# Six small edits at the seams of a two-layer-type network: the root's chain kept together, a padding and some loads and stores moved between engines

## The chip, the cores and the metric

The kernel runs on one core of a Trainium2 chip. A core has a matrix engine (TensorE, PE in the profile; PEld are its weight loads), a vector engine (VectorE, DVE), an activation engine (ScalarE, ACT), a general engine (GpSimd, POOL) and a sequencer for transfers (SyncE, SP). SP, ACT and POOL each have a queue into which they issue DMA transfers, and the transfers of all of them run on the core's 16 DMA engines. The metric is the device time of one execution in microseconds (us); the time before is the median of three runs, 2985.52 us (2983.61 to 2987.02).

## The reference, cut to what matters

The input is a sequence of 2048 positions with 640 channels. Four layers follow one another, each with a layer norm in front and a residual add behind: a long convolution (A), a multi-query attention (B), and the same two again with the same weights.

```python
x = A_u
x = x + _A_ref(_layernorm(x), ...)      # y = irfft(rfft(u, 2L) * rfft(K, 2L))[:L] + u * Dskip
x = x + _B_ref(_layernorm(x), wq, wk, wv, wo)
x = x + _A_ref(_layernorm(x), ...)      # the same K
x = x + _B_ref(_layernorm(x), wq, wk, wv, wo)

def _layernorm(x, axis=-1, eps=1e-5):
    m = jnp.mean(x, axis=axis, keepdims=True); v = jnp.var(x, axis=axis, keepdims=True)
    return (x - m) / jnp.sqrt(v + eps)

# A: K[d, l] = Re sum_n C[d,n] * exp(dt[d] * A[d,n] * l) * dt[d] * B[d,n],   128 states n, 2048 steps l
# B: 32 query heads of 20 channels, one key head and one value head of 20 channels
#    softmax(q k^T / sqrt(20)) v, the heads joined, times wo (640 x 640)
```

## The kernel before, in words

**Stages.** `kgen` makes the convolution kernel K in 20 units and writes it to the tensor `kd` in DRAM. `conv_layer` transforms K once into a spectrum (`kernel_spectra`, first layer only), then transforms x in five chunks of 128 channels, multiplies, and transforms back into `self.x`, which stays on the chip throughout ([128 partitions, 16 tiles, 640 channels]). `_attn` projects x to q, k and v in four blocks of 512 rows, then `main_loop` goes over 4 blocks (nb) x 8 head groups of four heads (hg) x 16 key tiles (t). Layers are called a, b, c, d.

**Order.** Tile, the layer that the kernel is written in, places each instruction by a planner with a cost model; inside a `manual_schedule` block the named engines keep the order in which the program writes them. The convolution is written out for PE, ACT and DVE; `kgen`'s loop too; `main_loop` for PE and ACT; `prepare(0)` of the attention for ACT and DVE (L1193). Everything else, the queues of SP and POOL among it, is in the planner's order. An engine runs its instructions in order: a waiting one holds up those behind it.

**The end of `kgen` (L567 to L569).** After unit 20 is begun, the tables' memory is released and `conv_weights` (L585) loads the forward transform weights `wf`, eight transfers of 512 KB, in GpSimd's queue. [...] SP's queue has the stores of K (L499): eight after unit 15, eight after the last unit.

**The end of a convolution (L957 to L1003).** When chunk 3 is under way, ScalarE computes mean and variance over the first 384 channels (`stats_first`, sums over an activation); in the first layer the attention's weights are split on the way into a high and a low part (`attn_weights`, six pieces: piece 0 are key and value weights in the padded tile `kv`, pieces 1 to 5 rows of wq; a first half casts and multiplies on PE, a second half writes the low part). Four `turn`s add the last chunk's inverse transform, four tiles at a time. After each turn `stats_last` takes bn_stats over the last 256 channels of these four tiles and aggregates them (eight operations); `norm_part` joins both parts and makes scale and shift. Its `root` (L734) is one square root on ACT and five dependent DVE operations, of which the reciprocal is the first, and one more product gives the shift. For block 0 (`norm_part(0, 1)`) the first six operations run after turn 0, and the other six are woven one by one between the eight operations of `stats_last(1)` (L998, L999).

**The start of an attention.** `prepare(nb)` normalizes four tiles on ACT (L1117), transposes them on PE in groups of two, two and one column blocks of 128 (L1128), copies the result to `xh` rounded (L1132, ACT) and the rest to `xl` (`low`, L1135, DVE). `norm_part(1, 3)`, the scale of blocks 1 to 3, stands around the first `low` of block 0. `project(nb)` multiplies with high and low weights (L1152), 15 matmuls for each of six column blocks, evicts q (L1164 to L1166), and calls `prepare(nb + 1)` at the third. `ob`, cast at L1098, is the operand that sums squares per head (L1179).

**The main loop.** Each step multiplies scores, exponentiates on ACT (L1286) and multiplies with the values (L1296). When a head group ends it is normalized, its rows go by DMA into `ot` chunks of 128 channels, and each chunk complete by then puts eight units (nb, k, u) on the list `later`. At t = 8 of each head group `later` moves to `queue`, and at t = 2, 5, 8, 11 and 13 one unit is taken from it: a product with `wo` on PE (L1356) and an add on DVE (L1344). What is left after the last step is multiplied in the tail. In layer d a tile that is complete is stored, one half by SP and one by GpSimd (L1351).

Of the kernel before, what the change touches and what calls it, by code (L numbers as in the profile page):

```python
# [11 lines left out]
F32 = mybir.dt.float32  # L12
# [3 lines left out]
AF = mybir.ActivationFunctionType  # L16
# [5 lines left out]
P = 128  # L22
# [173 lines left out]
class Net:  # L196
# [154 lines left out]
    def _kgen(self, ctx):  # L351
        tc, nc, ins = self.tc, self.nc, self.ins
# [152 lines left out]
        n = len(units)  # L505
        engines = {mybir.EngineType.PE, mybir.EngineType.Activation, mybir.EngineType.DVE}
        with tc.manual_schedule(engines=engines):
            for h in range(2):
                phase(0, h)
            for u in range(n + 3):  # L510
                now, nxt, prod, tot = u < n, u + 1 < n, 0 < u <= n, 2 <= u < n + 2
                odd = u % 2 == 1
                if u >= 3:
                    store(u - 3)
                if now and not odd:
                    trig(u, 0)
                if prod:
                    products(u - 1, 0)
                if now:
                    sizes(u, 0)  # L520
                    if odd:
                        exps(u, 0)
                if nxt:
                    phase_first(u + 1, 0)
                if tot:
                    sums(u - 2, range(0, 2))
                if now:
                    sizes(u, 1)
                    if odd:
                        exps(u, 1)  # L530
                if tot:
                    sums(u - 2, range(2, 3))
                if nxt:
                    phase(u + 1, 0)
                if now and odd:
                    sizes(u, 2)
                    exps(u, 2)
                if prod:
                    products(u - 1, 1)
                if now:  # L540
                    trig(u, 0 if odd else 1)
                if tot:
                    sums(u - 2, range(3, 5))
                if nxt:
                    phase(u + 1, 1)
                if prod:
                    products(u - 1, 2)
                if tot:
                    sums(u - 2, range(5, 7))
                if now:  # L550
                    if odd:
                        trig(u, 1)
# [12 lines left out]
                for t in {n: range(8, 12), n + 1: range(12, 16)}.get(u, ()):  # L565
                    self.stats(t)
                if u == n:  # L567
                    early.close()
                    self.conv_weights(nc.gpsimd)  # L569

    def conv_setup(self, ctx):
        tc = self.tc
# [110 lines left out]

    def stats_setup(self, nm):

        self.sm = {n: self.cvp.tile([P, 16], F32, name=f"sm{n}{nm}") for n in ("sum", "shift", "sq", "base")}
        self.mvb = self.cvp.tile([P, 16, 2], F32, name=f"mvb{nm}")

    def stats_first(self, g, dump):

# [102 lines left out]
    def conv_layer(self, nm, first):  # L793
# [7 lines left out]
        with tc.manual_schedule(engines={mybir.EngineType.PE, mybir.EngineType.Activation,  # L801
# [193 lines left out]
            for g in range(4):  # L995
                if g > 0:
                    turn(g)
                among = part[6:] if g == 1 else ()  # L998
                weave(self.stats_last(g), [(min(n + 1, 8), a) for n, a in enumerate(among)])  # L999
                if g == 0:  # L1000
                    part = self.norm_part(0, 1)
                    for call in part[:6]:
                        call()  # L1003
# [9 lines left out]
    def attn_weights(self, scr, fresh):  # L1013
# [11 lines left out]
                nc.sync.dma_start(w, dst.rearrange("p (k n) -> p k n", k=5))  # L1025
            return []
        kv = wp.tile([P, 5, 52], F32, name="kv")
        nc.gpsimd.memset(kv, 0.0)
        nc.sync.dma_start(kv[:, :, 0:20], ins["B_wv"].rearrange("(k p) n -> p k n", p=P))
        nc.sync.dma_start(kv[:, :, 32:52], ins["B_wk"].rearrange("(k p) n -> p k n", p=P))  # L1030
        minus = scr[:, 2688:2816]
# [27 lines left out]
                for w, dst in parts:  # L1059
                    nc.sync.dma_start(dst.rearrange("p (k n) -> p k n", k=5), w)  # L1060

        return [(lambda k=k: first(k), lambda k=k: second(k)) for k in range(6)]

    def attn_layer(self, nm, out=None):
        with ExitStack() as ctx:
# [16 lines left out]
    def _attn(self, ctx, nm, out):  # L1082
# [12 lines left out]
        ob = ap.tile([P, 6, 64], F32R, name="ob")  # L1095
        obr = ap.tile([P, 6, 64], F32, name="obr")
        nc.sync.dma_start(obr.rearrange("p m h -> p (m h)"), ins["c_ob"])
        nc.vector.tensor_copy(ob, obr)  # L1098
        nc.sync.dma_start(self.mxd.rearrange("h r n -> (h r) n"), ins["c_row"])
        nc.sync.dma_start(kt[1:66:64].bitcast(F32), self.mxd[32])  # L1100
        self.qps = {}
# [1 line left out]
        with tc.tile_pool(name=f"pj{nm}", bufs=1, reuse_waits="tile") as pj:  # L1103
# [7 lines left out]
            def prepare(nb):  # L1111

                xs = []
                for i in range(4):
                    t = 4 * nb + i
                    x = pj.tile([P, D], F32, tag="x", bufs=4, name=f"x{nb}{i}")
                    nc.scalar.activation(x, self.x[:, TAUS[t]], AF.Identity, scale=self.rs[:, t : t + 1],  # L1117
                                         bias=self.nmr[:, t : t + 1])
                    xs.append(x)
                if nb > 0:  # L1120
                    xhs[nb] = pj.tile([P, 5, 512], F32R, tag=f"xh{nb % 2}", bufs=1, name=f"xh{nb}")
                xh = xhs[nb]
                xl = xls[nb] = pj.tile([P, 5, 512], F32R, tag="xl", bufs=2, name=f"xl{nb}")
                for k0, n in ((0, 2), (2, 2), (4, 1)):
                    pt = self.ps2(f"pt{nm}{nb}{k0}")
                    for k in range(n):
                        for i in range(4):
                            nc.tensor.transpose(pt[:, 512 * k + 128 * i : 512 * k + 128 * i + 128],  # L1128
                                                xs[i][:, 128 * (k0 + k) : 128 * (k0 + k) + 128], self.ident)
                    hi, lo = xh[:, k0 : k0 + n], xl[:, k0 : k0 + n]  # L1130
                    pv = pt[:, 0 : 512 * n].rearrange("p (k c) -> p k c", k=n)
                    nc.scalar.activation(hi, pv, AF.Copy)  # L1132

                    def low(hi=hi, lo=lo, pv=pv):
                        nc.vector.tensor_tensor(lo, pv, hi.bitcast(F32), ALU.subtract)  # L1135

                    weave([low], [(0 if n < 6 else 1, a) for n, a in enumerate(
                        self.norm_part(1, 3) if nb == k0 == 0 else ())])

            def project(nb):  # L1140
                cols = slice(512 * nb, 512 * nb + 512)
# [48 lines left out]
                    call()  # L1190
                nc.vector.reduce_max(nrm[:, nb : nb + 1], pn, axis=AX.X)

            with tc.manual_schedule(engines={mybir.EngineType.Activation, mybir.EngineType.DVE}):  # L1193
                prepare(0)
            for nb in range(4):
                project(nb)
# [48 lines left out]
    def main_loop(self, ap, mp, kt, vt, nm, out):  # L1245
# [93 lines left out]
        def add(nb, u, py, last):  # L1339
# [7 lines left out]
            if out is None:  # L1347
                self.stats(t)
            else:
                for jh, eng in enumerate((nc.sync, nc.gpsimd)):  # L1350
                    eng.dma_start(self.rows(out)[jh][:, t], self.x[64 * jh : 64 * jh + 64, t])  # L1351

        def product(py, o, w, u, m, start, stop):
# [2 lines left out]
                nc.tensor.matmul(py[j : j + m], o[:, 128 * i + j : 128 * i + j + m],  # L1356
                                 w[:, 320 * half : 320 * half + 320], start=start, stop=stop)

        def projection(t):

            if t == 8:
                queue.extend(later)
                later.clear()
            if t in (2, 5, 8, 11, 13) and queue:
# [5 lines left out]
        with tc.manual_schedule(engines={mybir.EngineType.PE, mybir.EngineType.Activation}):  # L1370
# [3 lines left out]
            for s, step in enumerate(steps):  # L1374
# [4 lines left out]
                projection(t)  # L1379
# [110 lines left out]
```

## Time and profile before

One execution was profiled: 2985.19 us, with a span of 2983.4 us from the first to the last instruction. DVE, ACT, PE are busy times in us; the last two columns are the granted TensorE clock and the mean busy share of the DMA engines.

| stage | from, to (us) | PE | DVE | ACT | PE clock | DMA |
|---|---|---|---|---|---|---|
| kernel K | 0 to 284.6 | 169.04 | 265.66 | 226.36 | 0.67 | 0.31 |
| to the first spectrum matmul | 284.6 to 301.4 | 8.32 | 13.49 | 10.74 | 0.67 | 0.93 |
| spectra, convolution a | 301.4 to 602.9 | 280.66 | 285.46 | 112.38 | 0.97, 0.93 | 0.57, 0.46 |
| seam to attention b | 602.9 to 610.2 | 4.96 | 6.72 | 5.79 | 1.00 | 0.01 |
| projection b | 610.2 to 712 | 99.51 | 30.13 | 44.64 | 1.00 | 0.37 |
| main loop b | 722 to 1667 | 940.37 | 260.12 | 942.05 | 1.00 | 0.11 |
| projection d | 1906.5 to 2008.5 | 99.62 | 30.10 | 44.63 | 1.00 | 0.37 |
| main loop d | 2018 to 2964.7 | 941.95 | 244.09 | 942.16 | 1.00 | 0.11 |
| tail | 2964.7 to 2983.4 | 12.09 | 8.23 | 0.00 | 0.96 | 0.23 |

Over the span PE is busy 2774.5 us (93%), ACT 2425.9 (81%), DVE 1373.9 (46%), POOL 91.6 (3%). These shares are means over stages with different limits. A row of a timeline gives the start, the duration, the engine, the line, the operation and its tiles (buffer numbers left out, so both layers' tiles differ only in the letter behind the name), and in brackets how long the engine stood idle before it and what ended that. Matmuls are pipelined, so a PE row's end is modelled. SPq and POOLq rows are issues of transfers, not the transfers.

### The profile page before, as it was taken

How to read it: one execution, taken by the hardware profiler on the slowest of the kernel's cores; microseconds unless marked ns; L12 is line 12 of the kernel's file. 1: busy time of each engine (PE TensorE's matmuls, PEld its weight loads, DVE VectorE, ACT ScalarE, POOL GpSimd, SP SyncE). 2: the span in 40 equal slices, each digit the busy share in tenths (PEclk: the TensorE clock that was granted, in tenths of full speed). 3: DMA queues.
4: the chain of work that ended last, by engine and by line, in shares of the span. 5: the costliest groups of instructions: out<-in, count | busy, mean ns of one | idle time of the engine just before them, and what ended most of it. 6: DMA issues, size and time to landing. Idle time of an engine off the chain costs nothing. (4 is left out here: it accounts for less than half of the span.)

```text
span 2983.4 us, 52547 instructions
## 1 busy us (share of the span) xinstructions
PE 2774.5 (93%) x21712; PEld 1262.1 (42%) x21712; DVE 1373.9 (46%) x1800; ACT 2425.9 (81%) x2904; POOL 91.6 (3%) x153
## 2 busy tenths in 40 slices
PE   1776989998999999999999998899999999999999
PEld 0333978775232333333232687762233232323323
DVE  7999899942223222323232599721222222222222
ACT  5888243455999999999999634339999999999997
POOL 0001001100000000000000011000000000000000
PEclk9655999999999999999999999999999999999999
DMA  6113555533201010101100256231010101100100
GB/s 145 35 17 92 194 166 113 138 102 106 82 22 27 21 28 20 28 22 25 24 24 20 88 113 161 64 128 43 22 27 25 42 21 27 41 24 25 40 19 23
DMA packets 128112, 177.70 MB, mean 60 GB/s; under 512 B 59524, under 2 KB 84100, under 8 KB 124244
## 3 DMA queue, kind: packets, MB, share of 16 engines
q1 hardware_dynamic: 102680, 137.70, 16.1%
q0 software_dynamic: 23216, 35.55, 6.0%
q8 instruction: 175, 2.87, 0.4%
q10 hardware_dynamic: 1968, 0.98, 0.1%
q14 instruction: 73, 0.60, 0.1%
HBM read 95.22 MB, written 48.04 MB: 48 GB/s over the span
## 5 line engine op out<-in xcount | busy, mean ns | idle before, releaser
L1286 ACT ACTIVATE pt<-scd 128x1024 f32<-128x1024 f32 x1024 | 942.2, 1115 | 7.5 <-DMA qpd<-mxd 4.1
L1286 ACT ACTIVATE pt<-scb 128x1024 f32<-128x1024 f32 x1024 | 942.2, 1116 | 7.5 <-PE scb L1282 5.9
L1296 PE MATMUL pod<-pt,vt 128*32 128x512 f32 x4096 | 547.2, 606 | 4.4
L1296 PE MATMUL pob<-pt,vt 128*32 128x512 f32 x4096 | 547.0, 606 | 4.4
L1282 PE MATMUL scb<-qpb,kt 62*128 62x512 f32 x2048 | 386.0, 451 | 6.1 <-PEq L1231 5.7
L1282 PE MATMUL scd<-qpd,kt 62*128 62x512 f32 x2048 | 386.3, 452 | 5.7 <-DVEq L1231 5.3
L1282 PEld LDWEIGHTS scd<-qpd,kt 62*128 62x128 f32 x2048 | 166.1, 185 | 401.8 <-ACT pt L1286 392.9
L1282 PEld LDWEIGHTS scb<-qpb,kt 62*128 62x128 f32 x2048 | 166.0, 185 | 402.1 <-ACT pt L1286 392.5
L1344 DVE TENSOR_TENSOR x<-pyd,x 128x320 f32<-128x320 f32 x146 | 71.8, 492 | 561.0 <-PE pyd L1356 561.0
L1344 DVE TENSOR_TENSOR x<-pyb,x 128x320 f32<-128x320 f32 x146 | 71.8, 492 | 547.4 <-PE pyb L1356 547.4
L1316 DVE RECIPROCAL rc<-rc 128x512 f32<-128x512 f32 x62 | 207.9, 3353 | 2.1
L1296 PEld LDWEIGHTS pod<-pt,vt 128*32 128x32 f32 x4096 | 80.7, 108 | 178.3 <-issue 160.3
L1296 PEld LDWEIGHTS pob<-pt,vt 128*32 128x32 f32 x4096 | 80.6, 108 | 178.2 <-issue 160.1
L1356 PE MATMUL pyb<-wo,ot 128*32 128x320 f32 x1168 | 105.3, 432 | 0.0
L1356 PE MATMUL pyd<-wo,ot 128*32 128x320 f32 x1168 | 105.3, 432 | 0.0
L654 PE MATMUL za<-xna,wf 128*128 128x256 f32 x384 | 86.9, 389 | 4.9 <-ACT xna L821 4.9
L654 PE MATMUL zc<-xnc,wf 128*128 128x256 f32 x384 | 85.8, 385 | 5.0 <-ACT xnc L821 5.0
L1313 DVE COPY on<-pod 128x512 f32<-128x512 f32 x31 | 21.4, 691 | 136.1 <-PE pod L1296 122.1
L445 PE MATMUL pe<-kg,tm 48*128 48x512 bf16 (+1 forms) x120 | 61.1, 612 | 24.0 <-ACT m L453 15.3
L1313 DVE COPY on<-pob 128x512 f32<-128x512 f32 x31 | 21.4, 692 | 131.4 <-PE pob L1296 108.9
L654 PEld LDWEIGHTS za<-xna,wf 128*128 128x128 f32 x384 | 74.5, 195 | 16.6 <-ACT xna L821 6.2
L654 PEld LDWEIGHTS zc<-xnc,wf 128*128 128x128 f32 x384 | 73.7, 193 | 16.4 <-ACT xnc L821 6.2
(372 smaller groups left out, 3188.9 us busy)
## 6 DMA issues: line engine op xcount, KB each, us to landing
Akh<-kh SPq DMA_DIRECT2D x10, 2048.0 KB
kh<-Ak SPq DMA_DIRECT2D x5, 2048.0 KB
qhd<-qh SPq DMA_DIRECT2D x40, 256.0 KB
qld<-ql SPq DMA_DIRECT2D x40, 256.0 KB
qpb<-qhd SPq DMA_DIRECT2D x256, 40.0 KB
qpd<-qhd SPq DMA_DIRECT2D x256, 40.0 KB
ot<-on SPq DMA_DIRECT2D x216, 40.0 KB
wf<-in_c_wf POOLq DMA_DIRECT2D x16, 512.0 KB, 7.8
```

The source lines that it names most:

```text
L445: nc.tensor.matmul(pe[:, 512 * h : 512 * h + 512], grp(tm, u, par, rows), kg[0:rows, col : col + 512], start=True, stop=True)
L654: nc.tensor.matmul(zv[:, :, c, kk], self.wf[:, t + 4 * h, j, c, kk], x, start=(n == 0), stop=(n == 3))
L1282: nc.tensor.matmul(sc[:, 512 * par : 512 * par + 512], kt[rows, 128 * t : 128 * t + 128], qps[nb, hg, pr][rows], start=True, stop=True)
L1286: nc.scalar.activation(pt, sc, AF.Exp, scale=SCALE)
L1296: nc.tensor.matmul(po[32 * j : 32 * j + 32], vt[:, t], pts[step, j // 2][:, 512 * (j % 2) : 512 * (j % 2) + 512], start=(t == 0), stop=(t ...
L1313: nc.vector.tensor_copy(on, po)
L1316: nc.vector.reciprocal(rc, rc)
L1344: nc.vector.tensor_tensor(xh, py, xh, ALU.add)
L1356: nc.tensor.matmul(py[j : j + m], o[:, 128 * i + j : 128 * i + j + m], w[:, 320 * half : 320 * half + 320], start=start, stop=stop)
```

## The change

Six edits, in the order of the program:

- the forward weights `wf` are loaded in SP's queue at the end of `kgen`, not in GpSimd's (the second load, inside the first attention loop, stays in GpSimd's);
- the tiles of the statistics are allocated in the pool that lives on through the attention, and `stats_last(3)` moves into `prepare(0)`: two bn_stats ahead of the first `low` and two behind it, the aggregates behind the third `low`, then `norm_part(1, 3)`, then the cast of `ob`;
- of block 0's `norm_part`, the six operations from the reciprocal on run together ahead of `stats_last(1)`;
- the tile `kv` is no longer filled with zeros by GpSimd; ScalarE writes zeros into the twelve columns that no load fills; the six pieces are taken in the order 1, 2, 0, 3, 4, 5;
- the transposes of `prepare` go tile by tile, not column block by column block, and PE is among the engines whose order is kept for `prepare(0)`;
- in the last block of the main loop `later` moves to `queue` at t = 5, and the stores of the last block's second halves are issued by ScalarE.

```diff
-                    self.conv_weights(nc.gpsimd)
+                    self.conv_weights(nc.sync)
...
-        self.sm = {n: self.cvp.tile([P, 16], F32, name=f"sm{n}{nm}") for n in ("sum", "shift", "sq", "base")}
-        self.mvb = self.cvp.tile([P, 16, 2], F32, name=f"mvb{nm}")
+        self.sm = {n: self.xp.tile([P, 16], F32, tag=f"sm{n}", bufs=1, name=f"sm{n}{nm}") for n in ("sum", "shift", "sq", "base")}
+        self.mvb = self.xp.tile([P, 16, 2], F32, tag="mvb", bufs=1, name=f"mvb{nm}")
...
                 among = part[6:] if g == 1 else ()
-                weave(self.stats_last(g), [(min(n + 1, 8), a) for n, a in enumerate(among)])
+                if g < 3:
+                    weave(self.stats_last(g), [(0, a) for a in among])
...
-        nc.gpsimd.memset(kv, 0.0)
+        nc.scalar.activation(kv[:, :, 20:32], self.ident[:, 0:60].rearrange("p (k n) -> p k n", k=5),
+                             AF.Copy, scale=0.0)
...
-        return [(lambda k=k: first(k), lambda k=k: second(k)) for k in range(6)]
+        return [(lambda k=k: first(k), lambda k=k: second(k)) for k in (1, 2, 0, 3, 4, 5)]
...
-        nc.vector.tensor_copy(ob, obr)
...
-                    for k in range(n):
-                        for i in range(4):
+                    for i, k in ((i, k) for i in range(4) for k in range(n)):
...
-                    weave([low], [(0 if n < 6 else 1, a) for n, a in enumerate(
-                        self.norm_part(1, 3) if nb == k0 == 0 else ())])
+                    if nb > 0:
+                        low()
+                    elif k0 == 0:
+                        calls = self.stats_last(3)
+                        weave(calls[:2] + [low] + calls[2:4], ())
+                    elif k0 == 2:
+                        low()
+                    else:
+                        weave([low] + calls[4:], ())
+                        weave(self.norm_part(1, 3), ())
+                        nc.vector.tensor_copy(ob, obr)
...
-            with tc.manual_schedule(engines={mybir.EngineType.Activation, mybir.EngineType.DVE}):
+            with tc.manual_schedule(engines={mybir.EngineType.Activation, mybir.EngineType.DVE,
+                                             mybir.EngineType.PE}):
                 prepare(0)
...
-                for jh, eng in enumerate((nc.sync, nc.gpsimd)):
+                for jh, eng in enumerate((nc.sync, nc.gpsimd if nb < 3 else nc.scalar)):
...
-        def projection(t):
+        def projection(b, t):

-            if t == 8:
+            if t == (8 if b < 3 else 5):
```

More of the change, by code (lines that the diff above doesn't have):

```diff
@@ L1123, in prepare @@
                 xl = xls[nb] = pj.tile([P, 5, 512], F32R, tag="xl", bufs=2, name=f"xl{nb}")
+                calls = None
                 for k0, n in ((0, 2), (2, 2), (4, 1)):
                     pt = self.ps2(f"pt{nm}{nb}{k0}")
-                    for k in range(n):
-                        for i in range(4):
+                    for i, k in ((i, k) for i in range(4) for k in range(n)):
                             nc.tensor.transpose(pt[:, 512 * k + 128 * i : 512 * k + 128 * i + 128],
@@ L1378, in main_loop @@
                 values(step)
-                projection(t)
+                projection(nb, t)
                 if s + 2 < len(steps):
```

## The prediction

> **What bounds the kernel now.** I cut the span into stages first, with the table of windows (its columns: stage, length, then busy time and instructions of PE, PEld, DVE, ACT and POOL, then granted clock, DMA share and GB/s).
>
> ```profile
> 284.60:301.40 16.80, 8.32 (x333) 7.66 (x325) 13.49 (x22) 10.74 (x12) 8.02 (x14) 0.67 0.93 362
> 602.90:610.20 7.30, 4.96 (x46) 4.72 (x45) 6.72 (x27) 5.79 (x8) 0.00 (x0) 1.00 0.01 2
> 610.20:712.00 101.80, 99.51 (x459) 73.78 (x459) 30.13 (x47) 44.64 (x73) 0.00 (x0) 1.00 0.37 123
> 722.00:1667.00 945.00, 940.37 (x7302) 283.43 (x7299) 260.12 (x340) 942.05 (x1024) 7.19 (x20) 1.00 0.11 29
> 2964.70:2983.40 18.70, 12.09 (x48) 8.25 (x44) 8.23 (x12) 0.00 (x0) 2.11 (x4) 0.96 0.23 70
> ```
>
> The first attention loop has ACT busy 942.05 and PE 940.37 of 945.00 us; the second looks alike. Neither is touched, as shown under part 3. So the change can only act on four short seams: the start of the kernel spectra (284.6 to 301.4, DMA 93% busy), the two seams from convolution to attention (the one at 602.9 is shown; only DVE is busy nearly throughout), and the tail. Behind such a seam stands a stage without slack, the projection with PE busy 99.51 of 101.80 us, so a microsecond won or lost at its start is kept.
>
> **Part 1: forward weights issued by SyncE.** The timelines of POOL, SP, PE and DVE around 284 to 331 us (start, duration, engine, line, tile; in brackets the idle time before and what ended it):
>
> ```profile
> 284.64 4.26 POOL L598 DMA_DIRECT2D wf<-in_c_wf  x8 [9.66 <-PE pe L445]
> 293.06 0.58 POOL L782 DMA_DIRECT2D Rk<-kd  x1 [1.75 <-ACT c L437]
> 276.68 2.28 SPq L499 DMA_DIRECT2D kd<-kst  x2
> 300.44 1.06 SPq L499 DMA_DIRECT2D kd<-kst  x2
> 313.56 1.13 SPq L499 DMA_DIRECT2D kd<-kst  x1
> 301.40 6.85 PE L620 MATMUL zk<-Rk,wf 128*128 128x128 f32 x59 [1.67 <-DMA Rk<-kd]
> 331.34 2.29 DVE L633 TENSOR_TENSOR B<-Ak 128x2048 f32<-128x2048 f32 x1 [1.81 <-ACT Ak L622]
> 294.00:296.00 2.00, 0.21 (x8) 0.23 (x8) 2.00 (x3) 0.00 (x0) 0.54 (x1) 0.50 1.02 404
> ```
>
> The eight wf loads (4.19 MB) wait for the last sizes matmul, not for POOL, so their start stays near 284.6; what moves is the queue. SP is free: its earlier stores are issued by 278.96 (276.68 + 2.28) and the next start at 300.44. Behind wf on POOL stand the Dskip additions and the load Rk, and Rk's own release is ACT at 293. Rk takes 301.3 - 293.1 = 8.2 us to land, at 404 GB/s, where 1.05 MB alone would take 2.6 us: it stands behind wf. PE waits 1.67 us for it. [...] My estimate, from these rows: wf starts about 285.6 and at 404 GB/s has 0.8 MB left at 294.1, when Rk starts; at half rate each, wf needs 4 us, then Rk has 0.25 MB left: landing at 299 to 300. PE can gain at most its 1.67 us (before that it runs the last sums). Bounds: **1.67 gained, 0 if Rk lands no sooner**. I take 1.4. The gain passes on: DVE waits 1.81 us for ACT and PE's spectrum at 331.34, and from there is busy back to back. POOL's 4.26 us of issue is worth nothing by itself.
>
> [...]
>
> **Part 2: padding by ACT, other order of the pieces, in the first layer.**
>
> ```profile
> 551.99 0.42 ACT L1048 ACTIVATE wh<-kv 128x260 fp32r<-128x260 f32 x1 [13.10 <-DMA kv<-in_B_wk]
> 537.78 1.59 POOL L1028 MEMSET kv<- 128x260 f32 x1
> 577.73 0.60 ACT L878 ACTIVATE x<-ya 128x512 f32<-128x512 f32 x1 [1.73 <-PE ya L869]
> ```
>
> POOL's fill of 1.59 us goes; ACT gets one small fill (0.3 to 0.4 us) inside 13.10 us of idle time. The kv load can go out about 1.6 us sooner and, being third now, holds up fewer casts: ACT may run its statistics 2 to 3 us earlier. But at 577.73 ACT waits for PE anyway, and PE and DVE set the pace from there on. Both edits: **0**. If that cover were gone, at most the fill's 0.4 us would show; a gain above 0 has no waiter that I can name.
>
> **Part 3: the seam, the stores, the early projection.** First layer, engine timelines:
>
> ```profile
> 599.47 0.68 DVE L880 TENSOR_TENSOR x<-ya,x 128x512 f32<-128x512 f32 x1
> 602.62 0.16 DVE L732 TENSOR_TENSOR nmrna<-nm,rsna 128x4 f32<-128x4 f32 x1
> 610.05 0.22 DVE L739 RECIPROCAL rsna<-sq 128x12 f32<-128x12 f32 x1
> 611.13 0.17 DVE L732 TENSOR_TENSOR nmrna<-nm,rsna 128x12 f32<-128x12 f32 x1
> 602.88 3.36 ACT L1117 ACTIVATE x<-x,nmrna,rsna 128x640 f32<-128x640 f32 x4 [3.09 <-DVE nmrna L732]
> 605.51 2.35 PE L1128 MATMUL ptb<-ident,x 128*128 128x128 f32 x20
> 607.24 1.02 ACT L1132 ACTIVATE xh<-ptb 128x1024 fp32r<-128x1024 f32 x1 [1.00 <-PE ptb L1128]
> 606.43 1.40 DVE L709 BATCH_NORM_STATS2 sl<-x 128x6 f32<-128x256 f32 x4
> 607.75 0.36 DVE L710 BATCH_NORM_AGGREGATE mvba<-sl 128x2 f32<-128x6 f32 x4
> 608.92 1.22 DVE L1135 TENSOR_TENSOR xl<-ptb,xh 128x1024 fp32r<-128x1024 f32 x1
> 610.19 0.43 PE L1152 MATMUL pqb<-xh,wh 128*52 128x512 f32 x1 [2.34 <-DVE xl L1135]
> 612.49 0.43 PE L1152 MATMUL pqb<-xl,wh 128*52 128x512 f32 x1 [0.24 <-DVE xl L1135]
> 611.39 3.36 ACT L1117 ACTIVATE x<-x,nmrna,rsna 128x640 f32<-128x640 f32 x4 [1.02 <-DVE nmrna L732]
> 614.66 0.58 ACT L1164 ACTIVATE qh<-pqb 52x512 fp32r<-52x512 f32 x1
> 617.71 0.45 PE L1179 MATMUL pnb<-qs,ob 52*64 52x512 f32 x1
> ```
>
> The root chain of six operations undisturbed takes 1.25 us (610.05 to 611.30). Now it is spread among bn_stats and ends at 602.78; together, it starts when the residual add ends (600.15, with the gap of 0.1 seen) and ends at 601.5. ACT's normalization moves from 602.88 to 601.6 and ends at 604.96. The PE does its inverse transform until 605.5, then transposes at 0.118 us each (2.35 / 20); with the new order all inputs are there, the eight of the first tile end at about 606.6, and xh moves from 607.24 to 606.7 (done 607.7). DVE by then has done the last residual and two bn_stats (606.43 + 0.70 = 607.13), since the other two, the aggregates, five small operations and the ob cast were moved behind. So the first xl starts at 607.8, not 608.92: 1.1 us. The second one, after 1.22 + 0.70, is ready for PE's ninth matmul, so the 0.24 us goes too. **First layer: 1.35**.
>
> Second layer, the same rows:
>
> ```profile
> 1896.80 0.68 DVE L880 TENSOR_TENSOR x<-yc,x 128x512 f32<-128x512 f32 x1
> 1899.76 3.36 ACT L1117 ACTIVATE x<-x,nmrnc,rsnc 128x640 f32<-128x640 f32 x4 [2.64 <-DVE nmrnc L732]
> 1905.20 1.22 DVE L1135 TENSOR_TENSOR xl<-ptd,xh 128x1024 fp32r<-128x1024 f32 x1
> 1906.48 0.43 PE L1152 MATMUL pqd<-xh,wh 128*52 128x512 f32 x1 [1.89 <-DVE xl L1135]
> ```
>
> Here DVE is the limit. From 1897.58: chain 1.17 to the next issue, two groups of statistics (each 1.40 and 0.36, less what overlaps: 3.3 in all), two residuals (0.7 each), two bn_stats (0.7) put the first xl at about 1904.2; xh is there at 1903.9. That is 1.0, with the second wait **1.24**. Bounds for either seam: at best PE's whole wait (2.34 + 0.24 and 1.89 + 0.24), at worst the loss of rival 1.
>
> What is late next: the second half of the statistics. After low, aggregates (0.4), five operations (0.5), ACT's sqrt and the chain, the scale for blocks 1 to 3 comes at about 614.0, not 611.30, and ACT's next normalization starts at 614.15, not 611.39. PE transposes these blocks only some 10 us later. The ob cast, first read at 617.71, is done by 614.5. Moving the statistics' tiles to the pool that lives on issues nothing.
>
> The early projection is nothing at all. Units are popped first in, first out in five slots of each head group; in the last block the queue is never empty at a slot, with either step (from three units left of the block before, through 40 slots, to six of chunk 3 left over). The same unit stands in each slot, so no matmul and no wait moves: **0**.
>
> The tail, timeline and the DMA queues from 2973 on (packets, MB, share of 16 engines):
>
> ```profile
> 2974.51 3.42 SPq L1351 DMA_DIRECT2D out<-x  x4
> 2974.78 0.53 POOL L1351 DMA_DIRECT2D out<-x  x1 [162.61 <-DVE x L1344]
> 2977.73 0.53 POOL L1351 DMA_DIRECT2D out<-x  x1 [0.27 <-DVE x L1344]
> q1 hardware_dynamic: 320, 0.66, 23.3%
> q0 software_dynamic: 192, 0.66, 16.1%
> ```
>
> POOL issues 0.27 us after SP; ACT is idle here and could issue with SP. The queue of SP spends more engine time on as many bytes (23.3% against 16.1% of 11 us), so four more such stores may cost up to 0.8 us. I take **0.2 gained**, between 0.5 gained (POOL's issue time) and 0.8 lost, nearer the issue row since that is the one difference seen in order of time.
>
> **The sum.** 1.4 + 0 + 1.35 + 1.24 + 0 + 0.2 = 4.2 us. The profiled execution took 2985.19 us (span 2983.4 and 1.8 around it), 0.3 under the median of 2985.52. 2985.2 - 4.2 = **2981.0 us**.
>
> **Rivals.** (1) *ACT's order in the projection.* If the four normalizations stay ahead of qh (as at 611.39 and 614.66), ACT holds qh until 617.5, qs ends at 618.6, and PE's norms matmul, due at 616.1, waits until 618.7: a stall of 2.6 us, one later than today. In the second layer likewise, 1.1 later. For it: that is today's order. Against: today they fill idle time before qh is ready; then they would not be ready first, and outside the fixed region the planner decides. Sum: -1.4 - 0.2 + 1.0 + 1.1 = +0.5, **2985.7 us**. (2) *The loads are saturated, Rk lands no sooner* (DMA share 1.02 at 294 us): the sum without part 1, **2982.4 us**. (3) *Slower: wf behind the last kd stores on SP.* SP's order is the planner's too. Were wf queued behind stores that wait for ACT until 300.44 and issue until 314.7, the first wf tiles would land some 4 us later (my estimate: half of Rk's 8.2), near 318.7: 17 us after today's 301.4. With the other gains of 2.8, **2999 us**. It decides only if the order is so; wf is traced earlier and ready at 284.6, which speaks against.
>
> **How the numbers follow.** Forecast 0.63, rival 1 0.17, rival 2 0.12, rival 3 0.08. A measurement of this kernel tells about 0.2%, 6 us, from no change: faster means under 2979.5. The forecast alone reaches it, where seams take most of PE's wait (another 1.5 us): 0.18 of its chance. Slower, over 2991.5: rival 3, and 0.01 of rival 1. Same: the rest, 0.73. The range reaches from 2978.5 (forecast with the seams near their bound) to 2987.0 (rival 1 with the store's 0.8 lost and the runs' spread).
>
> **What would show it.** Part 1: wf issued by SP near 284.6, the first zk matmul at 299.8 to 300.2. Seams: the first projection matmul 1.0 to 1.2 us sooner against the end of the second residual add; qh before the normalizations, and no new wait at the norms matmul. Loops: as long as before. Wrong if zk starts at 301.4 or later, or if norms waits for qs.

## The result, and the profile after

The changed kernel takes **2981.69 us** (median of 18 runs, 2978.72 to 2982.69), and the kernel before, measured beside it, 2986.87 (18 runs). The ratio is **0.9981 [0.9975, 0.9988]**: 5.2 us less, between 3.6 and 7.5. That is just within the 0.2% that the prediction set as the bound to "faster". The profiled execution took 2980.52 us with a span of 2978.7; both are 4.7 under those of before.

Stages of the kernel after, from the table of windows (columns as in the prediction):

```profile
284.30:300.10 15.80, 8.72 (x337) 8.02 (x335) 12.53 (x20) 9.36 (x10) 1.59 (x3) 0.61 1.01 374
608.40:709.90 101.50, 99.41 (x459) 73.87 (x459) 31.94 (x59) 44.46 (x73) 0.00 (x0) 1.00 0.36 123
720.00:1665.00 945.00, 940.25 (x7308) 283.85 (x7310) 259.07 (x340) 942.44 (x1025) 7.65 (x21) 1.00 0.10 29
2960.30:2978.70 18.40, 13.00 (x52) 8.32 (x51) 8.23 (x12) 0.00 (x0) 0.00 (x0) 0.98 0.24 71
```

The loop needs the same 945 us and ACT the same 942 of it. The projection is 0.3 us shorter (608.4 to 709.9 against 610.2 to 712). The rest of the gain lies in the starts of the stages. Where it came from, by the same milestones in both traces (all from timelines; most of their rows stand below or in the prediction):

| milestone | before | after | after less before |
|---|---|---|---|
| first spectrum matmul (zk) | 301.40 | 300.09 | -1.31 |
| DVE's second whole butterfly | 331.34 | 330.83 | -0.51 |
| second residual addition, layer b | 599.47 | 598.87 | -0.60 |
| norms matmul, layer b | 617.71 | 615.50 | -2.21 |
| second residual addition, layer d | 1896.80 | 1894.78 | -2.02 |
| norms matmul, layer d | 1914.00 | 1910.39 | -3.61 |
| first of the last stores issued | 2974.51 | 2971.02 | -3.49 |
| end of the span | 2983.4 | 2978.7 | -4.7 |

So part 1 gave 0.5 in this execution, each seam 1.6, and the tail 1.2. Between these steps the two executions drift apart by up to 0.2 us.

**The start of the spectra**, timelines of POOL, SP, PE and DVE after:

```profile
281.82 0.70 POOL L782 DMA_DIRECT2D Rk<-kd  x1
284.26 5.27 SPq L598 DMA_DIRECT2D wf<-in_c_wf  x8
300.85 13.67 SPq L499 DMA_DIRECT2D kd<-kst  x8
300.09 15.35 PE L620 MATMUL zk<-Rk,wf 128*128 128x128 f32 x128
330.83 2.29 DVE L633 TENSOR_TENSOR B<-Ak 128x2048 f32<-128x2048 f32 x1 [1.80 <-ACT Ak L622]
```

The load Rk, the first load of K for the spectra, is no longer late: GpSimd issues it at 281.82 us, not 293.06, ahead of all of wf; it lands 5.3 us later, and PE begins without a wait. SyncE begins to issue the wf loads at 284.26, ahead of the last stores of K. Yet of PE's 1.31 us DVE gets 0.51.

**The seam of the first layer**, after:

```profile
598.87 0.68 DVE L880 TENSOR_TENSOR x<-ya,x 128x512 f32<-128x512 f32 x1
600.64 0.16 DVE L732 TENSOR_TENSOR nmrna<-nm,rsna 128x4 f32<-128x4 f32 x1
600.89 3.36 ACT L1118 ACTIVATE x<-x,nmrna,rsna 128x640 f32<-128x640 f32 x4 [1.70 <-DVE nmrna L732]
605.16 0.69 DVE L880 TENSOR_TENSOR x<-ya,x 128x512 f32<-128x512 f32 x1 [0.47 <-PE ya L869]
606.08 2.43 ACT L1133 ACTIVATE xh<-ptb 128x1024 fp32r<-128x1024 f32 x3 [1.83 <-issue]
607.14 1.22 DVE L1136 TENSOR_TENSOR xl<-ptb,xh 128x1024 fp32r<-128x1024 f32 x1 [0.50 <-ACT xh L1133]
608.42 0.43 PE L1162 MATMUL pqb<-xh,wh 128*52 128x512 f32 x1 [1.11 <-DVE xl L1136]
612.14 0.59 ACT L1174 ACTIVATE qh<-pqb 52x512 fp32r<-52x512 f32 x1 [0.25 <-PE pqb L1162]
613.27 1.74 ACT L1118 ACTIVATE x<-x,nmrna,rsna 128x640 f32<-128x640 f32 x2
615.50 0.44 PE L1189 MATMUL pnb<-qs,ob 52*64 52x512 f32 x1
```

Counted from the residual addition the shift is ready 1.4 us sooner (1.77 behind it, not 3.15), ACT normalizes from 600.89, and PE's wait ahead of the first product has gone from 2.34 to 1.11. The eviction qh (612.14) comes ahead of the next block's normalizations (613.27), and the norms matmul waits for nothing. The second layer has the same picture. Its norms matmul before, then the second residual addition, first product and norms matmul after:

```profile
1914.00 0.45 PE L1179 MATMUL pnd<-qs,ob 52*64 52x512 f32 x1
```

```profile
1894.78 0.68 DVE L880 TENSOR_TENSOR x<-yc,x 128x512 f32<-128x512 f32 x1
1903.28 0.43 PE L1162 MATMUL pqd<-xh,wh 128*52 128x512 f32 x1 [1.17 <-DVE xl L1136]
1910.39 0.45 PE L1189 MATMUL pnd<-qs,ob 52*64 52x512 f32 x1
```

**The tail**, timeline of the issues:

```profile
2971.02 3.42 SPq L1362 DMA_DIRECT2D out<-x  x4
2971.03 3.77 ACTq L1362 DMA_DIRECT2D out<-x  x4
```

From SyncE's first issue to the end of the span it is 7.68 us; before it was 2983.4 - 2974.51 = 8.89.

### The profile page after: what moved, and what is told of

It reads as the page before. It is cut to its first block, busy times and chain, and to the rows that moved or that the text cites. A ratio compares the mean times of both kernels' runs of the same rounds, so it can differ in the third digit from the quotient of the medians.

```text
span 2978.7 us, 52542 instructions
## 1 busy us (share of the span) xinstructions
PE 2771.9 (93%) x21712; PEld 1261.3 (42%) x21712; DVE 1374.8 (46%) x1800; ACT 2425.7 (81%) x2905; POOL 84.9 (3%) x140
```

## The experiments

Each ratio is to the kernel before, measured beside it on the same chip: 2986.7 us (33 runs) for the four parts alone; 2986.72 (21 runs) for the weights in four transfers, the 56 added matmuls, the root alone and the last tile's store; 2987.54 (13 runs) for the 27 added matmuls, the moved statistics and the first tile's store. Differences of a microsecond are hard to tell in whole times, so most verdicts rest on distances within one trace of each kernel.

### The four parts, each alone

**Forward weights by SyncE alone.**

```diff
-                    self.conv_weights(nc.gpsimd)
+                    self.conv_weights(nc.sync)
```

> The kernel before with one edit, the forward weights in SP's queue. Theory: the load Rk no longer stands behind wf, is issued near 282 instead of 293.06 and has landed long before PE is ready, so PE's wait of 1.67 us goes and the first zk matmul starts near 300.1; of that only some 0.5 us reaches DVE's second whole butterfly (331.34 before), because PE's clock rises later. Time: 0.5 us less (0.2 to 1.4). Rival (the place in memory, moved by the statistics' tiles, freed Rk): Rk is still issued near 293 and lands near 301, no gain.

Measured: 2984.5 us, ratio 0.9994 [0.9985, 1.0003]; the profiled execution 2984.92. Rk is issued at 282.32 and the spectrum matmul begins at 300.22 without a wait, but the butterfly comes no sooner than before (331.34). Windows from 298 us, and the butterfly's row:

```profile
298.00:300.00 2.00, 2.00 (x88) 2.00 (x80) 1.93 (x7) 0.00 (x0) 0.00 (x0) 0.50 0.93 360
300.00:302.00 2.00, 2.00 (x21) 1.70 (x13) 1.93 (x7) 1.62 (x2) 0.00 (x0) 0.64 1.02 385
331.50 2.29 DVE L633 TENSOR_TENSOR B<-Ak 128x2048 f32<-128x2048 f32 x1 [1.80 <-ACT Ak L622]
```

PE starts sooner, at half clock, and has lost the lead 31 us later. Part of that is a pause: after nine recorded matmuls PE stands idle for 0.49 us and goes on at 302.56. It is taken up below.

**The two seams alone** (the statistics' tiles, the root together, the moved statistics, the order of the transposes; all as in the diff of the change).

> The kernel before with the edits of the seam alone (statistics' tiles in the lasting pool, root's chain together, second half of the last statistics, scale and ob cast behind, transposes tile by tile, PE in the kept order). Theory: from the second residual add to the norms matmul 1.6 us less in each layer, 3.2 us in all; Rk as before. Rival (the seam's gain depends on the earlier clock or on the other edits): under 2 us.

Measured: 2982.82 us, 0.9989 [0.9980, 0.9998]; profiled 2981.55, 3.6 less than before. From the second residual addition to the norms matmul 16.65 us in the first layer (before 18.24) and 15.55 in the second (17.20): the two seams are worth 1.6 each, by themselves. The other traces agree: in the first layer this distance is 18.24 to 18.66 us in the five that have the seam as before, and 16.63 to 16.99 in the six that have all its edits.

One more thing differs between these traces. In four of the six with the old order of statistics (the root alone among them) the second layer's projection starts slowly (for about 3 us its matmuls start 0.43 us apart, then 0.23), and its norms matmul comes about 1 us later; 0.3 to 0.8 of that is left at the last stores. In the seven with the moved statistics they are 0.23 us apart from the second on; in the kernel after the granted clock is 1.00 there (1902 to 1912 us). PE's wait ahead of this projection is shorter in them (1.06 to 1.18 us, not 1.89 or more). Whether that is the reason was not tested.

**The last stores by ScalarE alone.**

```diff
-                for jh, eng in enumerate((nc.sync, nc.gpsimd)):
+                for jh, eng in enumerate((nc.sync, nc.gpsimd if nb < 3 else nc.scalar)):
```

> The kernel before with one edit, the four last stores issued by ScalarE. Theory from the two traces: the tail from the first tail product to the end is 1.2 us shorter, 0.1 to 0.3 of it before the last transfer ends and the rest after it. Rival (prediction): 0.2 us, all of it before the last transfer ends; the other 1 us in the changed kernel's span was a chance of one execution.

Measured: 2985.71 us, 0.9998 [0.9989, 1.0007]. The whole time can't tell it, the trace can: from the first issue (2976.09) to the end of the span (2983.8) it is 7.71 us, against 8.89 before and 8.75 to 8.9 in every other kernel whose last stores GpSimd issues.

**Padding, order of the pieces, projection from step 5, alone** (as in the diff of the change).

> The kernel before with the edits that were forecast at nothing: padding by ScalarE, the pieces' other order, the last block's projection from step 5. Theory: ACT's statistics run some 2 us earlier, the residual adds of the last chunk and everything behind stay, time within 0.3 us; every unit of the projection stands in the same slot. Rival: the earlier statistics let the inverse transform of chunk 3 start earlier, up to 1 us less.

Measured: 2987.09 us, 1.0003 [0.9994, 1.0012]. No stage of its trace is shorter by more than 0.3 us.

### Why Rk was late: the lane or the bytes ahead of it

In the program GpSimd's transfers use eight semaphores (lanes) in turn. In the program of the kernel before, Rk's wait list holds the semaphore of the third wf load, so GpSimd could not issue it before that had landed. That is a rival to "it stands behind wf in the queue". Loading the same bytes in four transfers takes the lane away and leaves the order.

```diff
+        if name == "c_wf" and self.rn is None:
+            for t in range(4):
+                eng.dma_start(w[:, t::4].rearrange("p h a b c k -> p h (a b c k)"),
+                              self.ins[name].rearrange("p (h t k) -> p h t k", h=2, t=4)[:, :, t])
+            return
         for t in (0, 4, 1, 5, 2, 6, 3, 7):
```

> The kernel before, but GpSimd loads the forward weights in four transfers of 1 MB (a tile and its partner) in place of eight of 0.5 MB: same queue, same bytes, same order. Theory A (Rk is held by a semaphore lane: among the eight lanes of GpSimd's transfers, used in turn, Rk's belonged to the third wf load, so GpSimd could not issue it before that load had landed, at 293.06 us): with four fewer transfers Rk falls on the lane of an old transfer, is issued at 286 to 288 us, and the first spectrum matmul has no wait on Rk: 299.8 to 300.3 us against 301.40. Theory B (my prediction's: Rk stands behind wf in the queue and its bandwidth): Rk lands after all of wf in any case, and the matmul starts at 301.0 or later with a wait of over 1 us. Theory C (only SyncE's ring lets it in): as B. Whole time by A: -0.5 to -1.5 us; by B and C within 0.5 us of before.

Measured: 2986.93 us, 1.0001 [0.9991, 1.0010]. Timelines of POOL and PE:

```profile
284.58 2.93 POOL L599 DMA_DIRECT2D wf<-in_c_wf  x4 [9.63 <-PE pe L445]
288.59 1.15 POOL L787 DMA_DIRECT2D Rk<-kd  x1
301.34 14.73 PE L625 MATMUL zk<-Rk,wf 128*128 128x128 f32 x128 [1.13 <-DMA Rk<-kd]
```

With half as many transfers Rk is issued sooner (288.59 against 293.06), and it does not matter: it lands at 301.3 us in both, 12.7 us after its issue here, 8.2 there. What makes it late are the 4.19 MB ahead of it, not the lane. In the kernel after, it goes 2.4 us *ahead* of wf, since the wf loads at the head of GpSimd's queue, which wait for PE, are no longer there. So the run after doesn't show whether a transfer of one queue can pass one of another; no run here had Rk behind wf in two queues.

### Where part 1's gain went: the clock, and a pause

From the first spectrum matmul to the butterfly, in every trace without extra matmuls, with the granted clock at 298 to 300 and at 300 to 302 us (from windows of each trace) and PE's idle time behind the first nine recorded matmuls:

| kernel | zk starts | clock 298, 300 | pause | butterfly | between |
|---|---|---|---|---|---|
| before | 301.40 | 0.74, 1.00 | | 331.34 | 29.94 |
| seams alone | 300.90 | 0.73, 1.00 | | 330.82 | 29.92 |
| stores alone | 301.57 | 0.50, 0.98 | | 331.49 | 29.92 |
| root alone | 301.40 | 0.50, 0.94 | | 331.31 | 29.91 |
| wf in four | 301.34 | 0.50, 0.86 | | 331.45 | 30.11 |
| pieces alone | 301.88 | 0.50, 0.50 | | 333.19 | 31.31 |
| moved statistics | 301.50 | 0.50, 0.50 | | 334.26 | 32.76 |
| after | 300.09 | 0.50, 0.55 | | 330.83 | 30.74 |
| wf alone | 300.22 | 0.50, 0.64 | 0.49 | 331.50 | 31.28 |
| last tile's store | 299.48 | 0.50, 0.99 | 1.40 | 331.35 | 31.87 |
| first tile's store | 299.58 | 0.50, 0.68 | 0.58 | 331.17 | 31.59 |

The last four have Rk early. Where PE does not pause, the stretch follows the clock: 29.9 us with the clock up by about 300, else 0.2 to 2.8 more. PE has been idle for over 6 us ahead of its last sums (6.21 to 7.15), and its clock is down there (0.50 at 296 to 298 in all of them). In five of the seven kernels that have Rk late it comes back during the last sums or PE's wait for Rk; in the four without that wait it is still 0.50 at 298 to 300, and the first spectrum matmuls run at half clock. When it comes back varies: the last sums begin between 295.1 and 295.8 in all, and in the 2 us from 298 the clock is 0.74 in the kernel before, while with the moved statistics it is still 0.50 at 304 to 306. What sets the moment was not shown.

The pause is a second cause. In the kernel with the last tile's store on GpSimd, PE does nine matmuls and then stands idle, with the clock at 0.99 from 300 to 302 and 1.00 behind that:

```profile
299.48 1.52 PE L620 MATMUL zk<-Rk,wf 128*128 128x128 f32 x9
302.41 9.76 PE L620 MATMUL zk<-Rk,wf 128*128 128x128 f32 x85 [1.40 <-issue]
```

In the three traces with a pause the butterfly comes 28.94 us behind its end; at full clock it comes 29.94 behind the first matmul, of which nine take 1.0. So the end of the pause decides when the butterfly comes. The profile names no releaser ("issue"); what PE waits for in the pause was not shown.

The changed kernel's own loss, 30.74 us against 29.94, has no pause in it. If the clock is its cause, matmuls that only keep PE busy must bring the gain back:

```diff
                     sums(u - 2, range(7, 8))
+                if u == n:
+                    warm = kp.tile([P, 1024], F32, tag="ph", bufs=1, name="warm")
+                    for i in range(56):
+                        nc.tensor.matmul(warm[:, 0:128], self.ident, self.ident, start=True, stop=True)
```

> The kernel after, with 56 matmuls added that compute nothing needed (the identity times itself, 128x128) in TensorE's idle stretch of 289.2 to 295.7 us. Theory A (part 1's gain of 1.3 us at the spectrum matmul reached VectorE as 0.5 us only since TensorE entered at half clock: granted 0.50 at 298 to 300 and 0.55 at 300 to 302 us, where the kernel before had 0.74 and 1.00): with the clock up, the last sums take half as long, the first spectrum matmul starts at 298.3 to 299.0 us, 128 of them take 13.8 us and not 15.35, and VectorE's second whole butterfly comes at 327.8 to 329.5 us, not 330.83. Whole time 1.3 to 3 us under the kernel after (2978.7 to 2980.4). Theory B (the loss is elsewhere, in VectorE's own chain or in the order of landing): the butterfly stays at 330.5 to 331 us and the time within 0.5 us of the kernel after.

Measured: 2985.53 us, 0.9995 [0.9986, 1.0005]. A mis-sized experiment: each of the 56 ran as two (the trace has 112 records), so they took 12 us and held the last sums back until 303.85. What it shows is the distance: zk at 305.78, butterfly at 335.72, 29.94 at full clock (1.00 from 290 us on). With 27:

> The kernel after with 27 such matmuls in place of 56: each ran as two, 0.107 us a half, so that 56 took 12 us and overran the idle stretch of 6.5 us; 27 take 5.8 us. From the first spectrum matmul to VectorE's second whole butterfly it was 29.94 us before, 30.74 after and 29.94 with the 56. Theory A (the clock): the matmul starts at 298.3 to 299.2 us, not 300.09, and the butterfly 29.9 us behind it, at 328.2 to 329.2, not 330.83. From there the gain stays, and the whole time is 1.3 to 2.6 us under the kernel after: 2979.0 to 2980.4 us, of the kernel before 0.9972 to 0.9980. Theory B: the last loads or VectorE's own chain (statistics until 308 us) set the butterfly: 330.5 to 331 us, and the time within 0.5 us of the kernel after.

Measured: **2979.08 us, 0.9975 [0.9965, 0.9985]**; profiled span 2976.2, 2.5 under the kernel after. Timelines of PE and DVE, and a window:

```profile
291.53 5.18 PE L563 MATMUL warm<-ident 128*128 128x128 f32 x44 [2.07 <-issue]
298.56 14.56 PE L624 MATMUL zk<-Rk,wf 128*128 128x128 f32 x128
328.50 2.29 DVE L637 TENSOR_TENSOR B<-Ak 128x2048 f32<-128x2048 f32 x1 [1.81 <-ACT Ak L626]
298.00:300.00 2.00, 2.00 (x59) 1.91 (x48) 1.93 (x7) 1.29 (x2) 0.00 (x0) 1.00 1.02 422
```

The clock is 1.00 from 290 us on, the last sums take half as long (their rows start 0.11 us apart, not 0.21), zk starts 1.5 us sooner still, and the butterfly comes 29.94 us behind it, 2.3 us ahead of the kernel after. That lies in theory A's range with some luck, for this execution was 0.8 us ahead before the added matmuls began (Rk issued at 281.04, not 281.82). Theirs are the other 1.5: 0.7 in the last sums and 0.8 in the stretch. A pause of 2.07 us now stands behind ten of the added matmuls, in the idle stretch, where it costs nothing. This version beats both kernels in the medians (8.5 us under before, against 5.2); the intervals of the two ratios overlap, so that it beats the kernel after rests on the trace.

### The seam: which of its edits does it

**The root together, alone.**

```diff
-                weave(self.stats_last(g), [(min(n + 1, 8), a) for n, a in enumerate(among)])
+                weave(self.stats_last(g), [(0, a) for a in among])
```

> The kernel before, with the root's six operations together ahead of the block's bn_stats, and nothing else of the seams: the second statistics stay ahead of the first subtraction, the transposes keep their order. By the prediction's sum both halves are needed: the chain's end moves from 602.78 to 601 us after a residual at 599.47, but VectorE still has 1.4 us of bn_stats, the aggregates and five small operations before the first subtraction. Theory A: from the second residual addition to the norms matmul 17.6 to 18.1 us in the first layer (18.24 before, 16.63 after) and 16.5 to 17.0 in the second (17.20 and 15.61). Theory B (the chain alone was the limit): 16.6 to 17.0 and 15.6 to 16.0.

Measured (one run, 2987.08 us): 18.39 us in the first layer and 18.79 in the second. Both theories miss: it gains nothing in the first layer and loses in the second. Of the 1.6 us lost there, 0.9 is the slow start of the projection (its first matmuls 0.43 us apart, not 0.23); 0.65 comes ahead of the first product, since DVE now waits out the root's chain instead of filling its gaps with statistics, and one operation of the root takes 0.48 us there, not 0.15 (see the last section). The last residual addition and the first product, DVE and PE:

```profile
606.76 0.69 DVE L880 TENSOR_TENSOR x<-ya,x 128x512 f32<-128x512 f32 x1 [0.47 <-PE ya L869]
609.97 1.22 DVE L1135 TENSOR_TENSOR xl<-ptb,xh 128x1024 fp32r<-128x1024 f32 x1
611.24 0.44 PE L1152 MATMUL pqb<-xh,wh 128*52 128x512 f32 x1 [2.34 <-DVE xl L1135]
```

From this residual to the product it is 4.48 us, as before (605.71 to 610.19), with the same wait of 2.34: between them DVE still does its statistics.

**The moved statistics alone** (with PE's order written out in the first block; the root interleaved and the transposes in the old order).

> The kernel before with the moved second statistics, constant cast and scale alone (and the order of TensorE written out in the first block): without the root together and without the transposes tile by tile. The root alone gave nothing (18.24 us from residual to norms in the first layer as before). Theory A (two branches meet at the first subtraction, VectorE's own work and ScalarE's normalization with the transposes; either change alone leaves the other branch): in the first layer the subtraction is held by the copy of the first transposes, done at 608.3 us by today's rows, not 608.92: 17.2 to 17.6 us from the second residual addition to the norms matmul; in the second, copy done 1904.99 against 1905.20: 16.6 to 17.0 us. Theory B (VectorE's work was the whole limit): 16.5 to 16.8 us and 15.5 to 15.8 us, as after.

Measured (one run, 2983.82 us): 17.46 us in the first layer, 16.58 in the second. Theory A: about half. DVE now waits for ACT ahead of the first subtraction,

```profile
609.94 1.23 DVE L1135 TENSOR_TENSOR xl<-ptb,xh 128x1024 fp32r<-128x1024 f32 x1 [0.96 <-ACT xh L1132]
```

because ACT's normalization is late without the root together (and by another 0.4 us in this trace, where one operation of the root took 1.01 us, not 0.60; see the last section). Two branches meet at the first subtraction, DVE's statistics and the chain root, normalization, transposes, copy. The first edit shortens only the second branch and gains nothing; the moved statistics shorten the first and gain 0.6 to 0.8; all edits together gain 1.6. What the new order of the transposes adds was not separated from the root.

### The tail: ScalarE's issue or GpSimd's landing

One of eight stores back on GpSimd, of the last tile, and in the other kernel of the first:

```diff
-                for jh, eng in enumerate((nc.sync, nc.gpsimd if nb < 3 else nc.scalar)):
+                for jh, eng in enumerate((nc.sync, nc.gpsimd if nb < 3 or i == 3 else nc.scalar)):
```

> The kernel after, with one of the eight last stores back on GpSimd: the half of the last tile. From the first of the last stores' issue to the span's end it was 8.89 us before (four stores by GpSimd), 7.68 after (none), and 7.71 with the stores alone by ScalarE. Theory A (the program's end waits longer for a transfer of GpSimd's queue): 8.6 to 9.0 us, with one as with four. Theory B (four stores on each of two queues that share the work differently; the gain is ScalarE's earlier issue): 7.6 to 8.0 us.

> The kernel after, with the half of the first of the last four tiles stored by GpSimd: its transfer lands some 3 us before the last one. With the half of the last tile on GpSimd the tail was 8.73 us, without any 7.68. Theory A1 (what costs is that a transfer of GpSimd's queue lands last): 7.6 to 8.0 us. Theory A2 (any store that GpSimd issues in the tail costs it, whenever it lands): 8.5 to 9.0 us.

Measured (one run each, 2982.47 and 2981.1 us): the tail is **8.73 us** with the last tile's half on GpSimd (2971.97 to 2980.7) and **7.95** with the first tile's (2971.35 to 2979.3). Windows near the end; of the kernel before, then of the first of these two:

```profile
2979.00:2980.00 1.00, 0.00 (x0) 0.00 (x0) 0.00 (x0) 0.00 (x0) 0.00 (x0) 1.00 0.85 287
2980.00:2981.00 1.00, 0.00 (x0) 0.00 (x0) 0.00 (x0) 0.00 (x0) 0.00 (x0) 1.00 0.20 79
```

```profile
2977.00:2978.00 1.00, 0.00 (x0) 0.00 (x0) 0.00 (x0) 0.00 (x0) 0.00 (x0) 1.00 0.84 307
2978.00:2979.00 1.00, 0.00 (x0) 0.00 (x0) 0.00 (x0) 0.00 (x0) 0.00 (x0) 1.00 0.00 0
```

Windows of 0.1 us put the last bytes at 2980.4 and 2977.9, and the span ends 3.0 and 2.8 us later. After, nothing moves from 2977.0 on and the span ends 1.7 later:

```profile
2976.00:2977.00 1.00, 0.00 (x0) 0.00 (x0) 0.00 (x0) 0.00 (x0) 0.00 (x0) 1.00 0.82 307
2977.00:2978.00 1.00, 0.00 (x0) 0.00 (x0) 0.00 (x0) 0.00 (x0) 0.00 (x0) 0.92 0.00 0
```

From the first issue to the last byte it is 5.9 to 6.0 us in all three, so the gain is not in the transfers. The end of the program comes 1.0 to 1.2 us later when GpSimd's queue carries the last store, alone or with three others, and 0.3 later when its store lands some 3 us before the last one (theory A1). What the program waits for in that time the trace doesn't show.

## Why the prediction was right, and where it was not

The time came within 0.7 us of the forecast, and the change is within 0.2%, as forecast. But two of its terms were wrong by about a microsecond each, in opposite directions, so that the sum came out so close is luck. The change itself was 5.2 us in the medians, where 4.2 was forecast; the kernel before was 1.35 us slower in them than in the runs that the prediction started from.

- **Part 1, forecast 1.4, measured 0.5 in this execution and about nothing over all.** The matmul started where the text said (300.09 in 299.8 to 300.2). Two steps failed. "Rk's own release is ACT at 293" and the estimate of two streams at half rate each: it was released at 281.82, ahead of wf, and landed long before it was needed. No run shows the half rate that the 1.4 us was worked out with: in the kernel after Rk's queue moves bytes alone from 284 to 286 us, both move some from 286 to 287 (0.15 and 0.21 MB), and wf's alone from there to 296. And "The gain passes on": PE's clock took 0.8 of it, and in three other traces the clock and the pause took all. Counted over all traces without extra matmuls, leaving out two in which the clock stayed down until 304 us or later, the butterfly comes at 331.28 in the mean of five with Rk late and at 331.21 in the mean of four with Rk early. Counted from the start of the last sums, which lie ahead of both, it is 35.69 and 35.77 us: no gain. Both left out have Rk late (333.19 and 334.26); with them the butterfly's gain is 0.8, and whether PE's wait made the low clock likelier there stays open. The window table had shown the clock (0.50 at 294 us, in the prediction's own fence), and the sum took PE's time behind its start as fixed.
- **Rival 2** (Rk lands no sooner) is false, yet its sum, 2982.4 us without part 1, lies as near to the measured median as the forecast's 2981.0. The new issuer changed the *order* of the transfers: Rk, issued 2.4 us ahead of wf, landed 5.3 us after its issue, not 8.2.
- **Part 2 and the early projection, forecast 0**: 1.0003 [0.9994, 1.0012] alone.
- **The seams, forecast 1.35 and 1.24, measured 1.6 and 1.6.** The mechanism and the branch that limits were right. The first product came 1.2 us sooner against the residuals in both layers (forecast 1.1 and 1.0; last residual to product 4.48 to 3.26 in the first, second residual to product 9.68 to 8.50 in the other). The rest is the second wait: the row shows 0.24, and the starts of the matmuls around it show more, 0.64 us from 611.85 to 612.49 where the others are 0.23 apart. That is 0.41, for a row's wait is counted from the modelled end of a pipelined matmul (rows of 0.39 to 0.43 us, starts 0.23 apart). Start to start would have given it.
- **Rival 1** (the normalizations stay ahead of qh) is false: qh at 612.14, normalization at 613.27, no wait at the norms matmul. **Rival 3** is false: wf was issued at 284.26, the last stores at 300.85.
- **The tail, forecast 0.2 between 0.5 gained and 0.8 lost, measured 1.1 to 1.2 gained.** Outside its bounds. The step that failed is to price the edit by issue and transfer alone. What lies between the last byte and the end of the span, 3.0 us before and 1.7 after, was no term, and it depended on the queue.

In sum 0.5 + 1.6 + 1.6 + 1.2 = 4.9 against 4.2 forecast and 4.7 in the profiled executions.

## What to carry to other kernels

A wait that was removed in front of a PE at half clock was worth less here than the row said (1.31 us at the first matmul, 0.51 at the butterfly, with the clock at 0.50 and 0.55): look at the granted clock on both sides, look for a pause behind the start that moved (0.49 to 1.40 us in three traces), and compare a later milestone, not that start. Two branches that meet at one instruction must be shortened together; the one edit that looked like the core of this seam gained nothing alone. Read the time between the last byte and the end of the span as a stage of its own, and of pipelined matmuls the distance of starts, not the wait in the row.

## What the runs showed of the hardware

**The idle stretch ahead of the last sums.** With 27 matmuls that compute nothing in an idle stretch of 6.5 us, the granted clock was 1.00 from 290 us on (without them 0.50 from 292 to 300), and DVE's butterfly came 1.5 us sooner against the start of wf's and Rk's loads; the profiled execution was 2.5 us shorter (2978.7 to 2976.2), 0.8 of it before these matmuls began.

**One DVE operation ended with a fill of GpSimd's.** The one TENSOR_SCALAR of the root takes 0.15 to 0.17 us, or 0.34 to 1.01, and in the traces of before, of after, of the root alone and of the moved statistics the long ones end when a fill of GpSimd does. GpSimd's two fills of kt, 1.40 us each, and DVE's operation, before and after, first layer:

```profile
599.56 2.79 POOL L1094 MEMSET kt<- 1x1536 f32 x2
601.78 0.60 DVE L742 TENSOR_SCALAR sq<-sq 128x4 f32<-128x4 f32 x1
```

```profile
599.01 2.79 POOL L1096 MEMSET kt<- 1x1536 f32 x2
600.07 0.34 DVE L742 TENSOR_SCALAR sq<-sq 128x4 f32<-128x4 f32 x1
```

Before, both end at 602.4 (599.56 + 2.79 and 601.78 + 0.60); after, the operation ends with the first fill, at 600.4. With the moved statistics alone it took 1.01 us and ended with the second fill as well (604.2). The reciprocal and the products next to it take 0.14 to 0.17 us during the fills. In the second layer of the kernel before, where both fills are over at 1898.44, the operation starts at 1899.11 and takes 0.15. No run here took the fill away, so this rests on the times that coincide. In the changed kernel it adds 0.17 us to the root in the first seam, where DVE waits 0.47 us for PE behind it anyway, and 0.3 in the second (0.48, not 0.16), where DVE is busy from there to the first subtraction.
